# Sinkhorn-sorted block attention with a SwiGLU block on one core: first weight loads in two pairs, mixing matrices of batches 1 to 3 on GpSimd, and a reordered start

## The chip, the cores and the metric

The kernel runs on one core of one Trainium2 chip. The metric is the device time of one execution in microseconds; three executions took 245.49, 244.75 and 244.44, median 244.75. Engines are named TensorE (PE; its weight loads PEld), VectorE (DVE), ScalarE (ACT), GpSimd (POOL) and SyncE (SP). SBUF is the on-chip working memory, PSUM the accumulators that TensorE writes, in eight banks of 2 KB per partition.

## The reference

There are 4 batches, 8 heads, 768 positions and 64 channels per head. The positions are cut into 8 blocks of 96. An 8x8 matrix P per batch and head is normalised five times by rows and columns, and mixes the blocks of keys and values; attention then runs inside each block. The result is the input of a gated block with 512 inputs and 1536 hidden units.

```python
P = sort_net
for _ in range(5):
    P = np.exp(P - np.max(P, axis=-1, keepdims=True))
    P = P / (np.sum(P, axis=-1, keepdims=True) + 1e-09)
    P = P / (np.sum(P, axis=-2, keepdims=True) + 1e-09)
k_sorted = np.einsum('bhij,bhjcd->bhicd', P, k_b)      # k in 8 blocks of 96
v_sorted = np.einsum('bhij,bhjcd->bhicd', P, v_b)
attn = softmax(scale * q_b @ k_sorted.T)               # 96 x 96 in each block
x = (attn @ v_sorted)                                  # -> 3072 tokens x 512
g, val = x @ w_gate, x @ w_val
out = (g * sigmoid(g) * val) @ w_out
```

## The kernel before

**Tiles.** The rows of one batch are 64 = 8 heads times 8 blocks (`R`), so two sets of rows fill the 128 partitions (`lowr`, `highr`). Inputs are float32 in HBM; GpSimd's DMAs convert them to bf16 on the way. P becomes a mixing matrix per batch: `w_ps` (a PSUM bank, 128 x 8 x 4 x 8, written by 32 small matmuls, L497) holds P of all four batches, and `mix_rows` (L501) multiplies it by a 0/1 mask of heads into `rmix[0]`, `rmix[1]` and `rmix["p"]` (batches 2 and 3). Matmuls with these matrices transpose and mix at once: `k0_chunk` (L280) gives the keys of batch 0, `q0_chunk` (L271) its queries, `v_chunk` (L295) its values; `kq_chunk` (L260) does keys and queries of batch 1 and later. Each chunk fills one PSUM bank (8 columns) or a pair (16), which VectorE or ScalarE then drains to SBUF (`drain`, L242: "v" or "s"). For two of the short key chunks the first 16 of 32 key parts are drained at once and the rest by a second drain (`parts`, `drain_rest`).

**Units.** A unit is a pair of heads and four blocks: `qk` makes eight score matmuls (L334) and the exponentials on ScalarE (`exps`, L345 and L347), `av` (L350) eight matmuls with a column of ones for the sum, then on VectorE a reciprocal (L365) and a product (L367) into `st`. Transposes by TensorE (`x_to`, L375) bring `st` into the layout `xts` that the gates read; ScalarE or VectorE drain them. The first half of batch 0 is four units; when these are transposed (`x_first`, L536) the gated block can begin.

**Gated block.** The tokens come in 8 half batches of 384. For each, 12 blocks of 128 hidden units: `gate` (L408) and `value` (L426), four matmuls of 384 columns each, tanh on ScalarE, two products on VectorE; then `outp` (L440) with w_out. The first two blocks are issued piece by piece in `early` (L546), as the transposed units arrive. The rest is a list (`ffn`, L619) into which the attention of the next half batches is merged at written times (`merge`, L606).

**Order.** The order on TensorE, GpSimd, VectorE and ScalarE is the order of the program in the start (`manual_schedule`, L154), and on all but VectorE later on. PSUM is shared by tags: "a" and "b" are two banks each, "x" one, "gen" three, and a chunk waits until its bank is drained. `w_ps` is in a "gen" bank. `fill` (L477) issues idle matmuls between dependent steps.

**Loads.** GpSimd issues the loads in order, with its own work between: v of batch 0, the identity, q and k of batch 0, three copies of v into `vch` (channels first), then the weights `load_gv(0, 512)` (gate and value, columns 0 to 511, one DMA each, L134), the second part of q (`load_q0(1)`), two more pairs of weight loads, v of batch 1 (`load_v`, L126), keys and queries of batch 1 (four loads, L100), w_out in three loads (L187), the copies of v of batch 1 (L632). At most eight of these DMAs are open; the ninth is issued when the first has landed.

Of the kernel before, what the change touches and what calls it, by code (L numbers as in the profile page):

```python
# [10 lines left out]
BF16 = mybir.dt.bfloat16  # L11
AF = mybir.ActivationFunctionType
ALU = mybir.AluOpType
# [4 lines left out]
def kernel(  # L18
# [11 lines left out]
    nc = tc.nc  # L30

    B, H, S, D = q.shape
    NB = sort_net.shape[-1]
# [10 lines left out]
    R = H * NB  # L44
# [7 lines left out]
    wo_dram = moe_w_out.rearrange("(mc p) f -> p mc f", p=128)  # L52

    const = ctx.enter_context(tc.tile_pool(name="const", bufs=1))
# [19 lines left out]
    wo_sb = [wpool.tile([128, 4, DM], BF16, name=f"wo{n}") for n in range(3)]  # L74
# [24 lines left out]
    def load_groups(tile4, rows, src, lo, hi):  # L99
        nc.gpsimd.dma_start(out=tile4[rows, lo:hi, 0:GC * D],  # L100
                            in_=src[:, lo * GC:hi * GC, :].rearrange("p (s c) d -> p s (c d)", c=GC))

    def kq_tile(b):
        if b not in kq_tiles:
            kq_tiles[b] = nat_tile(natp, f"kq{b}", "nat")
        return kq_tiles[b]
# [4 lines left out]
    def load_k(b, lo, hi):  # L111
        load_groups(kq_tile(b), highr, k_nat[b], lo, hi)
# [5 lines left out]
    def load_q(b, lo, hi):  # L118
        load_groups(kq_tile(b), lowr, q_nat[b], lo, hi)
# [13 lines left out]
    def load_w(sb, dram, lo, hi):  # L133
        nc.gpsimd.dma_start(out=sb[:, :, lo:hi], in_=dram[:, :, lo:hi])  # L134

    def load_gv(lo, hi):
        load_w(wg_sb, wg_dram, lo, hi)
        load_w(wv_sb, wv_dram, lo, hi)

    def copy_v(eng, pair, rows, s, n=4, d0=0, d1=D):  # L140
        cs = slice(s * (C // n), (s + 1) * (C // n))
        dst = vch3[rows, d0:d1, cs]
        src = (dense(v_tiles[0])[rows, cs, d0:d1] if rows == lowr else
               grouped(v_tiles[pair])[rows, s, :, d0:d1])
        if eng is nc.scalar:
            eng.copy(dst, src.transpose([0, 2, 1]))  # L146
        else:
            eng.tensor_copy(dst, src.transpose([0, 2, 1]))  # L148

    ident = const.tile([128, 128], BF16)  # L150
    lowr, highr = slice(0, R), slice(R, 2 * R)
# [7 lines left out]
    halves = (lowr, highr)  # L159
# [5 lines left out]
    def load_q0(t):  # L165
        nc.gpsimd.dma_start(out=q0[t].rearrange("p c d -> p (c d)"), in_=q_runs[0, t])
# [7 lines left out]
    copy_v(nc.gpsimd, 0, lowr, 0)  # L174
    copy_v(nc.gpsimd, 0, lowr, 3)
    copy_v(nc.gpsimd, 0, lowr, 5, 8, 40, D)
    load_gv(0, 512)
    load_q0(1)
    load_gv(512, 1024)
    load_gv(1024, DF)  # L180
    load_v(1, 0, 2)
    load_v(1, 2, 4)
    for lo, hi in ((0, 2), (2, 4)):
        load_k(1, lo, hi)
        load_q(1, lo, hi)
    for n in range(3):
        nc.gpsimd.dma_start(out=wo_sb[n], in_=wo_dram[:, n * 4:(n + 1) * 4, :])  # L187

    rmix = {b: const.tile([128, 2, H, NB], BF16, name=f"rmix{b}") for b in (0, 1, "p")}
    for t in rmix.values():  # L190
# [14 lines left out]
    mask = const.tile([128, H], BF16)  # L205
# [3 lines left out]
    rowreds = [const.tile([BH, NB, 1], FP32, name=f"rowred{it}") for it in range(N_ITER)]  # L209
    colred = const.tile([BH, 1, NB], FP32)  # L210
    p_bf = const.tile([BH, NB, 4, NB], BF16)
    def pair_tile(name, tag):
        return psum.tile([128, 1024], FP32, name=name, tag=tag)

    def bank_tile(name, tag="gen"):
        return psum.tile([128, 512], FP32, name=name, tag=tag, bufs=3 if tag == "gen" else 1)
# [54 lines left out]
    def q0_chunk(t, at, n, eng, tag):  # L271
        dst = kqt_tile(0)[:, GI * C:2 * GI * C].rearrange("p (g t r c) -> p t g r c", g=H2, t=2, c=QC)[:, t]
        tp = chunk_tile("tq0", n // 8, tag).rearrange("p (l g r) -> p l g r", l=n, g=H2)
        for lc in range(n):
            for two in range(2):
                nc.tensor.matmul(tp[two * D:(two + 1) * D, lc], lhsT=q0[t][:, at + lc, :],
                                 rhs=sel[:, two], start=True, stop=True)
        drain(eng, dst[:, :, :, at:at + n], tp.rearrange("p l g r -> p g r l"))

    def k0_chunk(at, n, eng, tag, parts=None):  # L280
        dst = kqt_tile(0)[:, 0:GI * C].rearrange("p (n a c) -> p a n c", a=2, c=HC)
        rm = rmix[0].rearrange("p a (g two) i -> p two a g i", two=2)
        tp = chunk_tile("tk0", n // 8, tag).rearrange("p (l a n) -> p l a n", l=n, a=2)
        for lc in range(n):
            for two in range(2):
                nc.tensor.matmul(tp[two * D:(two + 1) * D, lc].rearrange("p a (g i) -> p a g i", g=H2),
                                 lhsT=k0[:, at + lc, :], rhs=rm[:, two], start=True, stop=True)
        src = tp.rearrange("p l a n -> p a n l")
        if parts is None:
            drain(eng, dst[:, :, :, at:at + n], src)  # L290
            return
        drain(eng, dst[:, :, 0:parts, at:at + n], src[:, :, 0:parts])
        return lambda e: drain(e, dst[:, :, parts:, at:at + n], src[:, :, parts:])

    def v_chunk(b, at, n, eng, tag):  # L295
        rows = slice(0, 128) if b % 2 else lowr
        dst = vt_tile(b // 2)[:, b % 2]
        mix = rmix[b][rows, 0].rearrange("p a b -> p (a b)")
        tp = chunk_tile("tv", n // 8, tag).rearrange("p (l n) -> p l n", n=H * NB)
        for ld in range(n):  # L300
            col = (at + ld) * C
            nc.tensor.matmul(tp[:, ld, :], lhsT=vch[rows, col:col + 128], rhs=mix,  # L302
                             start=True, stop=True)
        drain(eng, dst[:, :, at:at + n], tp[0:C].transpose([0, 2, 1]))
# [45 lines left out]
    def qk(b, u, tag="b"):  # L350
        exps(b, u, *scores(b, u, tag))

    def av(b, u, tag="a"):
        half, g = divmod(u, H2)
        vt = vts[b // 2][:, b % 2].rearrange("p (h i) e -> p h i e", h=H)
        av_ps = pair_tile("av_ps", tag).rearrange("p (two n) -> p two n", two=2)
        o = av_ps.rearrange("p two (i e) -> p two i e", i=4)
        for two in range(2):
            e = es[(b, u)][two]
            for i4 in range(4):  # L360
                nc.tensor.matmul(o[:, two, i4, 0:D + 1], lhsT=e[:, i4 * C:i4 * C + 128],  # L361
                                 rhs=vt[:, 2 * g + two, half * 4 + i4, 0:D + 1],
                                 start=True, stop=True)
        r_sb = ssp.tile([C, 2, 4, 1], FP32, name="r_sb", tag="r")
        nc.vector.reciprocal(r_sb, o[0:C, :, :, D:D + 1])  # L365
        st = ssp.tile([C, 4, 2, D], BF16, name="st", tag="st")
        nc.vector.tensor_tensor(st.rearrange("p i two d -> p two i d"), o[0:C, :, :, 0:D],  # L367
                                r_sb.to_broadcast([C, 2, 4, D]), op=ALU.mult)
        sts[(b, u)] = st
# [105 lines left out]
    idle_ps = bank_tile("idle_ps", "x")  # L475

    def fill(tile, n):  # L477
        for _ in range(n):
            nc.tensor.matmul(tile, lhsT=warm_sb[:, 0:128], rhs=warm_sb, start=True, stop=True)  # L479
# [13 lines left out]
    w_ps = bank_tile("w_ps")[:, 0:NB * B * H].rearrange("p (i b h) -> p i b h", b=B, h=H)  # L493
# [4 lines left out]
                             lhsT=p_bf[:, i].rearrange("p a b -> p (a b)"),  # L498
                             rhs=ident[0:BH, 0:BH], start=True, stop=True)

    def mix_rows(dst, rows, b):  # L501
        nc.vector.tensor_tensor(dst, mask[rows].unsqueeze(2).to_broadcast([R, H, NB]),
                                w_ps[rows, :, b].transpose([0, 2, 1]), op=ALU.mult)

    mix_rows(rmix[0][lowr, 0], lowr, 0)
    mix_rows(rmix[0][highr, 1], highr, 0)
    q0_chunk(0, 0, 16, "s", "b")
    v_chunk(0, 0, 8, "v", "gen")
    v_chunk(0, 8, 8, "s", "gen")
    v_chunk(0, 16, 16, "v", "a")  # L510
    v_chunk(0, 32, 8, "v", "gen")
    v_chunk(0, 40, 16, "s", "b")
    v_chunk(0, 56, 8, "s", "gen")
    q0_chunk(0, 16, 8, "v", "x")
    k0_chunk(0, 16, "s", "a")
    k0_chunk(16, 16, "v", "b")
    rest = [k0_chunk(at, 8, "s", "gen", 2 * NB) for at in (32, 40)]
    for drain_rest in rest:
        drain_rest("v")
    idle_ps = bank_tile("idle_ps", "x")  # L520
    fill(idle_ps, 3)
    qk(0, 0, "a")
    qk(0, 1, "b")
    for b in range(1, B):
        rows = halves[b % 2]
        mix_rows(rmix["p"][rows, b % 2] if b > 1 else rmix[1][rows, 0], rows, b)
    qk(0, 2, "gen")
    fill(idle_ps, 1)
    av(0, 0, "a")
    fill(idle_ps, 2)  # L530
    av(0, 1, "b")
    xts[(0, 0)] = xtp.tile([128, H2, TW], BF16, name="xt0_0", tag="xt")
    qk(0, 3, "mixed")
    av(0, 2, "a")

    def x_first(u, eng, tag):  # L536
        x_ps = xt_tile(tag, 1)[:, 0]
        x_to(x_ps, 0, u)
        drain(eng, xts[(0, 0)][:, u, :], x_ps.rearrange("p a b -> p (a b)"))

    x_first(0, "s", "gen")
    x_first(1, "s", "gen")
    av(0, 3, "b")
    first = {}
# [144 lines left out]
```

## Time and profile before

| what | us |
|---|---|
| median of three executions | 244.75 |
| the profiled execution | 245.05 |
| its span on the core | 243.1 |
| PE busy | 235.9 (97%) |
| DVE busy | 154.7 (64%) |
| ACT busy | 112.6 (46%) |
| POOL busy | 51.2 (21%) |
| DMA, mean over the span | 102 GB/s |

The profile is of one execution; times count from the start of its span. In the slices each digit is a fortieth of the span in tenths of busy time. A timeline line has the start, the length, the engine, the line of the kernel, the operation, the tile written and those read, the shape, a count, and in brackets how long the engine stood idle before and what ended the wait. Lines of one kind on end are merged. GB/s count the bytes as written, in bf16 for the loads. PE is busy while matmuls overlap, so a busy PE is not one at its peak.

### The profile page before, as it was taken

The numbers are of one execution on the slowest core, as the hardware profiler recorded it, in microseconds if no ns is written. First come the engines' busy times: TensorE is split into PE (matmuls) and PEld (weight loads), VectorE is DVE, ScalarE is ACT, GpSimd is POOL, SyncE is SP. The second block draws the span as 40 slices with busy tenths as digits, with TensorE's granted clock in tenths as the row PEclk, the third lists the DMA queues.
The fourth block names the chain that finished last, engine by engine and source line by source line (L and its number), as shares of the span: only waits on it lengthen the run. The fifth ranks groups of instructions, "written<-read, shape, count | busy, mean of one in ns | idle before, by whom it ended". The sixth has DMA issues, their size and how long they took to land.

```text
span 243.1 us, 6156 instructions
## 1 busy us (share of the span) xinstructions
PE 235.9 (97%) x2613; PEld 138.7 (57%) x2613; DVE 154.7 (64%) x326; ACT 112.6 (46%) x191; POOL 51.2 (21%) x45
## 2 busy tenths in 40 slices
PE   8798999999999999999999999999999999999994
PEld 5375666676556556555555565565556555555543
DVE  6686789876665585866855855584576476445700
ACT  3976663486625544455453353254325434332312
POOL 5992229970006089000000000000000000000000
PEclk9999999999999999999999999999999999999999
DMA  5989999999926998553122212012111211110122
GB/s 101 210 121 206 207 212 212 205 210 192 166 78 99 220 176 118 108 107 68 48 73 58 49 47 80 0 59 63 32 43 48 74 36 43 43 43 3 43 86 86
DMA packets 39642, 24.77 MB, mean 102 GB/s; under 512 B 29376, under 2 KB 34368, under 8 KB 39616
## 3 DMA queue, kind: packets, MB, share of 16 engines
q0 software_dynamic: 19632, 14.16, 39.3%
q1 hardware_dynamic: 19840, 10.17, 15.7%
q8 instruction: 20, 0.33, 0.6%
q10 hardware_dynamic: 144, 0.07, 0.1%
q14 instruction: 6, 0.05, 0.1%
HBM read 28.32 MB, written 7.86 MB: 149 GB/s over the span
## 4 chain that ended last, share of the span: by engine, by line
PE 89%; DMA 7%; POOL 2%; DVE 1%; issue 0%; ACT 0%; POOLq 0%
PE v_ps L430 26%; PE g_ps L412 25%; PE o_ps L447 25%; DMA wv_sb<-in_moe_w_val_dram 4%; DMA v<-in_v_dram 3%; PE av_ps L361 3%; PE tkq L266 3%; PE qk L334 3%; POOL vch L148 1%; PE tv L312 1%; PE o_ps L463 1%; PE tv L302 1%; PE v_ps L551 1%; PE g_ps L551 1%; PE x_ps L378 0%
## 5 line engine op out<-in xcount | busy, mean ns | idle before, releaser
L422 DVE SCALAR_TENSOR_TENSOR gs_sb<-th_sb,g_ps 128x384 bf16<-128x384 bf16 x96 | 52.9, 551 | 50.3 <-ACT th_sb L420 47.3
L412 PE MATMUL g_ps<-xt,wg_sb 128*128 128x384 bf16 x376 | 76.6, 326 | 0.1
L430 PE MATMUL v_ps<-xt,wv_sb 128*128 128x384 bf16 x376 | 76.5, 326 | 0.0
L420 ACT ACTIVATE th_sb<-g_ps 128x384 bf16<-128x384 f32 x96 | 47.1, 491 | 56.8 <-PE g_ps L412 54.1
L447 PE MATMUL o_ps<-wo,h 128*128 128x512 bf16 x276 | 64.4, 379 | 0.0
L435 DVE SCALAR_TENSOR_TENSOR h<-v_ps,gs_sb 128x384 bf16<-128x384 f32 x96 | 53.4, 556 | 7.7 <-PE tkq L266 0.5
L412 PEld LDWEIGHTS <-wg_sb 128*128 128x128 bf16 x376 | 34.9, 97 | 23.4
L430 PEld LDWEIGHTS <-wv_sb 128*128 128x128 bf16 x376 | 35.0, 97 | 23.1 <-issue 0.2
L447 PEld LDWEIGHTS <-h 128*128 128x128 bf16 x276 | 26.0, 98 | 28.5
L452 ACT COPY o_sb<-o_ps 128x512 f32<-128x512 f32 x23 | 13.5, 586 | 49.3 <-PE o_ps L447 49.3
L148 POOL COPY vch<-v 64x1536 bf16<-64x1536 bf16 (+2 forms) x11 | 28.7, 2655 | 10.2 <-DMA v<-in_v_dram 10.2
L347 ACT ACTIVATE e_all<-qk 96x768 bf16<-96x768 f32 x30 | 23.2, 801 | 4.3 <-PE qk L334 4.3
L367 DVE TENSOR_TENSOR st<-av_ps,r_sb 96x512 bf16<-96x512 f32 x32 | 21.8, 680 | 0.3
L361 PEld LDWEIGHTS <-e_all 96*128 96x128 bf16 x256 | 11.9, 97 | 4.9 <-ACT e_all L347 0.6
L361 PE MATMUL av_ps<-vt,e_all 96*128 96x65 bf16 x256 | 13.0, 193 | 0.0
L246 ACT CAST vt<-tv 96x1024 bf16<-96x1024 f32 (+1 forms) x11 | 10.1, 931 | 4.7 <-PE tv L312 3.5
L365 DVE RECIPROCAL r_sb<-av_ps 96x8 f32<-96x8 f32 x32 | 6.4, 199 | 7.9 <-PE av_ps L361 7.9
L244 DVE CAST vt<-tv 96x1024 bf16<-96x1024 f32 (+1 forms) x7 | 7.4, 1065 | 2.2 <-PE tv L312 1.8
L479 PE MATMUL idle_ps<-warm_sb 128*128 128x512 bf16 x24 | 7.1, 408 | 0.0
L244 DVE COPY oq_v<-o_ps 128x128 f32<-128x128 f32 x1 | 0.3, 292 | 9.3 <-PE o_ps L463 9.3
L397 POOL DMA_DIRECT2D q_scr<-in_q_dram x2 | 5.6, 2810 | 0.3 <-issue 0.3
L146 ACT COPY vch<-v 64x768 bf16<-64x768 bf16 (+1 forms) x4 | 5.5, 1388 | 0.2 <-DMA v<-in_v_dram 0.2
(83 smaller groups left out, 130.4 us busy)
## 6 DMA issues: line engine op xcount, KB each, us to landing
out_dram<-o_sb SPq DMA_DIRECT2D x23, 256.0 KB, 2.0
v<-in_v_dram POOLq DMA_DIRECT2D x4, 384.0 KB, 13.1
wg_sb<-in_moe_w_gate_dram POOLq DMA_DIRECT2D x3, 512.0 KB, 11.7
wv_sb<-in_moe_w_val_dram POOLq DMA_DIRECT2D x3, 512.0 KB, 13.4
wo<-in_moe_w_out_dram POOLq DMA_DIRECT2D x3, 512.0 KB, 15.9
kqp<-in_k_dram POOLq DMA_DIRECT2D x2, 768.0 KB, 9.4
q_scr<-in_q_dram POOLq DMA_DIRECT2D x2, 768.0 KB, 17.5
v<-in_v_dram POOLq DMA_DIRECT2D x2, 768.0 KB, 9.8
```

The lines of the kernel that those rows point to most:

```text
L148: eng.tensor_copy(dst, src.transpose([0, 2, 1]))
L246: nc.scalar.copy(dst, src)
L347: nc.scalar.activation(e_all[:, n:n + 2, 0:4 * C], wide[0:C, :, 0:4 * C], AF.Exp, scale=scale)
L361: nc.tensor.matmul(o[:, two, i4, 0:D + 1], lhsT=e[:, i4 * C:i4 * C + 128], rhs=vt[:, 2 * g + two, half * 4 + i4, 0:D + 1], start=True, sto ...
L367: nc.vector.tensor_tensor(st.rearrange("p i two d -> p two i d"), o[0:C, :, :, 0:D], r_sb.to_broadcast([C, 2, 4, D]), op=ALU.mult)
L412: nc.tensor.matmul(g_ps, lhsT=wg_sb[:, kc, ts(m, 128)], rhs=xt[:, kc, :], start=(kc == 0), stop=(kc == NKC - 1))
L420: nc.scalar.activation(th_sb, g_ps, AF.Tanh, scale=0.5)
L422: nc.vector.scalar_tensor_tensor(gs_sb, th_sb, 1.0, g_ps, op0=ALU.add, op1=ALU.mult)
L430: nc.tensor.matmul(v_ps, lhsT=wv_sb[:, kc, ts(m, 128)], rhs=xt[:, kc, :], start=(kc == 0), stop=(kc == NKC - 1))
L435: nc.vector.scalar_tensor_tensor(h_tiles[n][:, m, :], v_ps, 0.5, gs_tiles.pop(m), op0=ALU.mult, op1=ALU.mult)
L447: nc.tensor.matmul(o_ps, lhsT=h_w[:, m, ts(t3, 128)], rhs=wo_sb[part][:, m % 4, :], start=(m == 0), stop=(m == NFC - 1))
L452: nc.scalar.copy(o_sb, o_ps)
```

## The change

Five things are changed, all in the start of the program. (1) The first pair of weight loads, columns 0 to 511 of gate and value, becomes two pairs of 256 columns with the second part of q between them. (2) `w_ps` of batches 1 to 3 is copied to SBUF (`w_sb`) by VectorE right after batch 0's two mixing matrices, and GpSimd makes the three other mixing matrices from the copy; before, VectorE made them from PSUM after the second unit's scores. In GpSimd's order they stand behind the loads of v of batch 1, and the loads of k and q of batch 1 and of w_out are moved behind them. (3) The chunks of batch 0 change order, size, bank and drain: the second q chunk moves ahead, the keys' second 16 columns become two chunks of 8 on ScalarE, the first part of the last key chunk is drained by VectorE, and the last value channels (56 to 63) come behind the keys, in bank "x", ahead of the remaining key drains. (4) The idle matmuls are fewer and elsewhere. (5) `av(0, 0)` comes ahead of `qk(0, 2)`, and `av(0, 2)` behind the first unit's transposes.

```diff
@@ -174,17 +174,13 @@
-    load_gv(0, 512)
+    load_gv(0, 256)
     load_q0(1)
+    load_gv(256, 512)
     load_gv(512, 1024)
     load_gv(1024, DF)
     load_v(1, 0, 2)
     load_v(1, 2, 4)
-    for lo, hi in ((0, 2), (2, 4)):
-        load_k(1, lo, hi)
-        load_q(1, lo, hi)
-    for n in range(3):
-        nc.gpsimd.dma_start(out=wo_sb[n], in_=wo_dram[:, n * 4:(n + 1) * 4, :])
@@ -209,6 +205,7 @@
+    w_sb = const.tile([128, NB, B, H], BF16)
@@ -498,40 +495,47 @@
-    def mix_rows(dst, rows, b):
-        nc.vector.tensor_tensor(dst, mask[rows].unsqueeze(2).to_broadcast([R, H, NB]),
-                                w_ps[rows, :, b].transpose([0, 2, 1]), op=ALU.mult)
-
-    mix_rows(rmix[0][lowr, 0], lowr, 0)
-    mix_rows(rmix[0][highr, 1], highr, 0)
+    def mix_rows(eng, dst, rows, w, b):
+        eng.tensor_tensor(dst, mask[rows].unsqueeze(2).to_broadcast([R, H, NB]),
+                          w[rows, :, b].transpose([0, 2, 1]), op=ALU.mult)
+
+    mix_rows(nc.vector, rmix[0][lowr, 0], lowr, w_ps, 0)
+    mix_rows(nc.vector, rmix[0][highr, 1], highr, w_ps, 0)
+    nc.vector.tensor_copy(w_sb[:, :, 1:], w_ps[:, :, 1:])
+    for b in range(1, B):
+        rows = halves[b % 2]
+        mix_rows(nc.gpsimd, rmix["p"][rows, b % 2] if b > 1 else rmix[1][rows, 0], rows, w_sb, b)
+    for lo, hi in ((0, 2), (2, 4)):
+        load_k(1, lo, hi)
+        load_q(1, lo, hi)
+    for n in range(3):
+        nc.gpsimd.dma_start(out=wo_sb[n], in_=wo_dram[:, n * 4:(n + 1) * 4, :])
+
     q0_chunk(0, 0, 16, "s", "b")
     v_chunk(0, 0, 8, "v", "gen")
     v_chunk(0, 8, 8, "s", "gen")
     v_chunk(0, 16, 16, "v", "a")
-    v_chunk(0, 32, 8, "v", "gen")
+    v_chunk(0, 32, 8, "s", "gen")
+    q0_chunk(0, 16, 8, "v", "x")
     v_chunk(0, 40, 16, "s", "b")
-    v_chunk(0, 56, 8, "s", "gen")
-    q0_chunk(0, 16, 8, "v", "x")
-    k0_chunk(0, 16, "s", "a")
-    k0_chunk(16, 16, "v", "b")
-    rest = [k0_chunk(at, 8, "s", "gen", 2 * NB) for at in (32, 40)]
+    k0_chunk(0, 16, "v", "a")
+    k0_chunk(16, 8, "s", "gen")
+    k0_chunk(24, 8, "s", "gen")
+    rest = [k0_chunk(32, 8, "s", "gen", 2 * NB), k0_chunk(40, 8, "v", "gen", 2 * NB)]
+    v_chunk(0, 56, 8, "v", "x")
     for drain_rest in rest:
         drain_rest("v")
-    idle_ps = bank_tile("idle_ps", "x")
-    fill(idle_ps, 3)
+    fill(pair_tile("idle_ps", "b")[:, 0:512], 2)
     qk(0, 0, "a")
     qk(0, 1, "b")
-    for b in range(1, B):
-        rows = halves[b % 2]
-        mix_rows(rmix["p"][rows, b % 2] if b > 1 else rmix[1][rows, 0], rows, b)
+    idle_ps = bank_tile("idle_ps", "x")
+    fill(idle_ps, 1)
+    av(0, 0, "a")
     qk(0, 2, "gen")
     fill(idle_ps, 1)
-    av(0, 0, "a")
-    fill(idle_ps, 2)
     av(0, 1, "b")
     xts[(0, 0)] = xtp.tile([128, H2, TW], BF16, name="xt0_0", tag="xt")
     qk(0, 3, "mixed")
-    av(0, 2, "a")
@@ -539,6 +543,7 @@
     x_first(0, "s", "gen")
+    av(0, 2, "a")
     x_first(1, "s", "gen")
     av(0, 3, "b")
```

## The prediction

> **What bounds the kernel now.** First the page's slices (40 slices of 6.08 us, busy tenths).
>
> ```profile
> PE   8798999999999999999999999999999999999994
> DVE  6686789876665585866855855584576476445700
> PEclk9999999999999999999999999999999999999999
> DMA  5989999999926998553122212012111211110122
> ```
>
> TensorE is full from the fifth slice on, at the full granted clock, and DMA is full from the third to the ninth. From about 26 us TensorE runs one written order without holes, so a microsecond won ahead of it is a microsecond of span, unless a later wait gives it back. The change touches only what lies ahead; next therefore the timeline of TensorE there (start, length, operation, count, idle before).
>
> ```profile
> 17.53 0.92 PE L334 MATMUL qk<-kqt 64*128 64x96 bf16 x24
> ...
> 18.77 0.42 PE L361 MATMUL av_ps<-vt,e_all 96*128 96x65 bf16 x8
> ...
> 21.48 0.32 PE L551 MATMUL g_ps<-xt,wg_sb 128*128 128x384 bf16 x1
> 22.39 0.34 PE L551 MATMUL v_ps<-xt,wv_sb 128*128 128x384 bf16 x1 [0.58 <-DMA wv_sb<-in_moe_w_val_dram]
> 22.56 0.34 PE L378 MATMUL x_ps<-ident,st 96*128 96x96 bf16 x4
> ...
> 23.46 0.33 PE L378 MATMUL x_ps<-ident,st 96*128 96x96 bf16 x4
> ...
> 25.46 0.32 PE L276 MATMUL tq<-sel,qk 128*64 128x64 bf16 x8
> ```
>
> The first value matmul waits for wv_sb, and queued behind it are the transposes of units 2 and 3. VectorE had their inputs (st) at 21.82 and 22.66, so unit 3's transpose at 23.46 is late through the weights alone. VectorE before it:
>
> ```profile
> 16.16 1.89 DVE L244 CAST kqt<-tk 128x1024 bf16<-128x1024 f32 x3 [0.31 <-PE tk L286]
> 18.07 0.23 DVE L502 TENSOR_TENSOR rmix<-mask,w_ps 64x64 bf16<-64x64 bf16 x1
> 18.31 0.45 DVE L502 TENSOR_TENSOR rmixp<-mask,w_ps 64x64 bf16<-64x64 bf16 x2
> 19.23 0.20 DVE L365 RECIPROCAL r_sb<-av_ps 96x8 f32<-96x8 f32 x1 [0.46 <-PE av_ps L361]
> ```
>
> The three mixing matrices end 0.46 us before av_ps comes: they delay nobody. Last, GpSimd's timeline, the landings of wg_sb and wv_sb after issue, and two later places where TensorE is not far behind a supplier.
>
> ```profile
> 12.79 0.79 POOL L134 DMA_DIRECT2D wg_sb<-in_moe_w_gate_dram  x1
> 13.56 0.76 POOL L134 DMA_DIRECT2D wv_sb<-in_moe_w_val_dram  x1
> 14.31 0.55 POOL L166 DMA_DIRECT2D qk<-in_q_dram  x1
> ...
> 36.96 0.74 POOL L187 DMA_DIRECT2D wo<-in_moe_w_out_dram  x1 [0.87 <-DMA v<-in_v_dram]
> 37.74 11.24 POOL L148 COPY vch<-v 64x1536 bf16<-64x1536 bf16 x4
> ```
> ```profile
> DMA to landing us min/median/max: 6.8/11.7/15.3
> DMA to landing us min/median/max: 8.8/13.4/18.0
> ```
> ```profile
> 30.40 0.81 PE L430 MATMUL v_ps<-xt,wv_sb 128*128 128x384 bf16 x4
> 50.23 0.63 PE L302 MATMUL tv<-rmix,vch 128*128 128x64 bf16 x16
> ```
>
> With the issue times: first wg_sb lands at 19.56, first wv_sb 22.34, second wv_sb 29.05. The matmul at 30.40 is the first to read that second part (1.3 us spare); the one at 50.23 needs GpSimd's four copies, which end at 48.92 (1.26 us spare).
>
> **The weights in two pairs.** By the packet records the queue moves 1024 B packets at 200 per us over 16 engines (79.8 ns each on its engine), 3072 B at 68 (235), 128 B at 1220 (13.1). A line through the first and last, 3.6 ns + 0.0744 ns/B, gives 232 for the third, so it holds. The new 512 B packets cost 41.7 ns; 2048 of them for 1024 old ones: 85.4 - 81.7 = 3.7 us over 16 engines, delta = 0.23 us later for everything behind. Ends: 0 (cost by bytes) and 5.1 us (512 B priced like 1024 B: 81.7/16). I take 0.23, as four sizes lie on its line.
> The first pair is now as many bytes as the first wg_sb alone: wv_sb lands at about 19.7 instead of 22.34. Issues: two more of 0.76 us on GpSimd, each far ahead of the bytes it queues. Only eight DMAs are ever open (each late issue waits for the landing eight before); counted through, every later issue waits for the same bytes as before, so all from the second gate pair on move by delta only.
> The Trainium skill (DMA: Bandwidth & Descriptors, Anatomy of one DMA) prices a GpSimd DMA at about 2.0 us + bytes/436e3; two more in series would be +4.0 us and a slower kernel. Landings at 26.54, 29.05 and 31.62 stand 2.5 us apart, which is 524 KB at 207 GB/s with no fixed part left, so I take nothing for it.
>
> **Mixing matrices on GpSimd.** VectorE loses 0.67 us that nobody waited for: gain 0. It gains a copy of 128x192 at 12.34; between the 64x64 row (0.22) and the 128x256 drain (0.415), at 1.06 ns per element 0.35. It ends at 12.69, before the first value drain can start (12.73): cost 0, at most 0.03. It frees w_ps's bank at 12.7 instead of 18.76, a third bank for the chunks. GpSimd's products show in no row: 0.25 (its select) to 2.8 us each (64x1536 copy), I take 0.5 by the 64x288 copy (0.66). They stand behind the second v issue (about 22.4) and ahead of the seven issues of k, q, wo (4.6 us); the last wo issue only becomes possible at 36.9, and the queue has bytes until 38.5. Even 8.4 us fits: cost 0.
> The Trainium skill (GPSIMD Engine Reference, Engine selection) sends elementwise products to VectorE, about 2x slower for two inputs on GpSimd. At 0.45 us each the sum stays as it is.
>
> **Drains reordered.** I walk the new order with the old durations (VectorE holds 1.14 us for a 1024 drain, 0.60 for 512, 0.33 for 256; ScalarE 0.91, 0.48, 0.27; matmuls 29 ns value, 16 ns k and q). VectorE: value 0 at 12.73, value 16 at 13.43, q to 15.17; k 0 has its bank at 14.70, is done at 15.40, drained 15.44 to 16.67. ScalarE: q to 13.31, value 8, value 32 to 14.26, value 40 14.51 to 15.42, k 16 from 15.68 to 16.27, k 24, k 32's first half to 17.03. The chunk k 40 waits for k 16's bank (16.27), is done at 16.77, its first half drained by VectorE at 17.23. Then qk(0,0) can start at 17.37 instead of 17.53: 0.16 earlier. Value 56 (to 17.83) and the rests (to 18.49) now stand behind the keys on VectorE; av(0,0) waits for its exp until 18.56, qk(0,2) starts at 18.87, so neither sees them. Ends: 0.15 later (k 40's drain behind value 56 by half its time) to 0.4 earlier (third bank and fewer fills pay in full).
>
> **Units and first gates.** exp(0,0) 17.76 to 18.56, av(0,0) 18.62, VectorE's reciprocal at 19.07 (was 19.23); its four rounds of 0.84 us end unit 3's st at 22.51 (was 22.66). The exps follow at 18.47, 19.25, 20.00. av(0,2), now behind the first transposes, runs at 20.2, ahead of VectorE's turn at 20.75: cost 0. The first value matmul (21.45) finds its weights. What is late next is st and the x bank, drained of unit 2 by ScalarE at 22.57: unit 3's transpose runs at 22.62 instead of 23.46. Gain 0.84; with qk(0,0) unmoved still 0.69.
>
> **Does it last.** The value matmuls come to 29.56, their weights land at 29.05 + 0.23; the q loads of batch 1 land at 41.65 + 0.23, wanted at 42.4; GpSimd's copies end at 49.15, wanted at 49.39. Each holds, the last by 0.24 us: it caps the gain at 1.26 - delta.
> Sum: -0.84 us. The profiled execution took 245.05 (span 243.1 and 1.95 around it), giving 244.2; the median is 0.30 below it: **243.9 us**.
>
> **Rivals.**
> *Small packets cost like large ones* (slower). Delta 5.1 us: the copies would end at 54.0 and the chunk at 50.23 comes 3.8 us late: 248.6. It decides from delta 1.26 us, 50 ns per 512 B packet. The 128 B row (13.1) speaks against it; that no 512 B row exists, for it.
> *The weights come no sooner.* First wg_sb's bytes at 207 GB/s would be through 2.4 us before its landing; if a small DMA's landing trails its bytes as far and more, wv_sb lands after 22 us and only a little is left: 244.3 to 244.8. That the first wg_sb, equal in bytes, landed at 19.56 speaks against it.
> *More is won.* If qk(0,0) comes 0.4 earlier, and delta is near 0, the gain is 1.1 to 1.26 us, where the copies cap it: 243.5. The third bank speaks for it, the two bank waits in my walk against it.
>
> **How the numbers follow.** Forecast 0.52 (own range 243.6 to 244.3), weights no sooner 0.15, small packets 0.14, more won 0.19. A measurement tells 0.5%, 1.2 us. Faster by more: the last case and the forecast's edge with the scatter of the runs (244.44 to 245.49), 0.25; slower 0.14; the rest, 0.61, within. The range runs from the cap with scatter (243.1) past no gain (245.2).
>
> **What would show it.** Right: no wait of the first value matmul for wv_sb, unit 3's transpose near 22.6, first w_ps copy under 0.42 us, the gates of the stream from 25.5, tv of batch 1 at 49.4. Wrong: a hole before the value matmuls near 29.6 or before tv, behind GpSimd's copies; qk(0,0) after 17.6; 512 B packets over 50 ns.

## The result and the profile after

The changed kernel took 245.34 us (median of 12, 245.15 to 245.85), the kernel before beside it 244.58 us (median of 12, 244.31 to 245.49). The ratio is 1.0029, with a 95% interval of 1.0019 to 1.0039: slower by 0.76 us. The prediction was 243.9 us, and its range ended at 245.2.

The profiled execution of the changed kernel took 245.19 us. Its slices (40 of 6.07 us, busy tenths) look like those of before.

```profile
span 242.8 us, 6133 instructions
...
PE   6798999999999999999999999999999999999994
...
PEclk9999999999999999999999999999999999999999
DMA  5999999999937997453122112012111211110122
```

TensorE is as full and its clock as high. The span of 242.8 us is even shorter than the 243.1 of the profile before, though the kernel is slower. Two things must therefore be kept apart: what lies around the span, and which execution of before is the yardstick. Next TensorE's timeline in the changed kernel (start, length, operation, count, idle before).

```profile
17.26 0.38 PE L476 MATMUL idle_ps<-warm_sb 128*128 128x512 bf16 x1 [0.16 <-issue]
17.57 0.52 PE L331 MATMUL qk<-kqt 64*128 64x96 bf16 x16
...
18.82 0.42 PE L358 MATMUL av_ps<-vt,e_all 96*128 96x65 bf16 x8 [0.41 <-ACT e_all L344]
...
21.67 0.32 PE L556 MATMUL g_ps<-xt,wg_sb 128*128 128x384 bf16 x1
21.84 0.32 PE L556 MATMUL v_ps<-xt,wv_sb 128*128 128x384 bf16 x1
...
22.90 0.33 PE L375 MATMUL x_ps<-ident,st 96*128 96x96 bf16 x4
...
24.91 0.95 PE L273 MATMUL tq<-sel,qk 128*64 128x64 bf16 x48
25.79 0.50 PE L409 MATMUL g_ps<-xt,wg_sb 128*128 128x384 bf16 x2
```

The first value matmul no longer waits for its weights, and unit 3's transpose comes at 22.90 instead of 23.46. Against the profile of before that is a gain of 0.55 us up to the gates' stream (the first gate matmul of the list behind `early`, at 25.79 us here and 26.34 there). But the kernel before, run again, shows in another execution (the same view):

```profile
17.55 0.92 PE L334 MATMUL qk<-kqt 64*128 64x96 bf16 x24
...
21.50 0.32 PE L551 MATMUL g_ps<-xt,wg_sb 128*128 128x384 bf16 x1
21.66 0.32 PE L551 MATMUL v_ps<-xt,wv_sb 128*128 128x384 bf16 x1
...
22.82 0.33 PE L378 MATMUL x_ps<-ident,st 96*128 96x96 bf16 x4
...
24.82 0.95 PE L276 MATMUL tq<-sel,qk 128*64 128x64 bf16 x48
25.70 0.50 PE L412 MATMUL g_ps<-xt,wg_sb 128*128 128x384 bf16 x2
```

Here no wait stands before the first value matmul: the first wv_sb landed at 20.86 us, not at 22.34. This is the usual execution. Of 147 executions of the kernel before that stood beside the experiments, 46 have a span of 243.0 us or more; most of the rest lie at 242.3 to 242.8. (Four slow ones, at a granted clock near 0.985, are left out.) The profile that the prediction was made from is one of the late ones.

Against the usual execution the change loses in three places, in us:

| place | before | after | loss |
|---|---|---|---|
| first mixing product (VectorE, 11.86 and 11.84) to the gates' stream | 13.84 | 13.94 | 0.10 |
| gates' stream to the first key chunk of batch 1 (42.62 and 42.92) | 16.92 | 17.13 | 0.21 |
| time outside the span (median) | 1.93 | 2.44 | 0.51 |

The three add up to 0.82 us, the difference of the two profiled executions (245.19 and 244.37); by the medians it is 0.76.

The second place is seen in the changed kernel's chain of waits (start, length, what).

```profile
24.65 0.33 PE v_ps L556 x2
24.98 0.64 PE tq L273 x32
25.62 0.01 issue
25.63 0.56 DVE h L432
26.19 0.47 DVE gs_sb L419
...
26.76 0.56 DVE h L432
27.32 0.61 DVE kqt L241
27.92 0.05 issue
27.97 0.52 PE qk L331 x16
28.48 0.02 issue
28.50 0.81 PE v_ps L427 x4
```

VectorE's first h product, its second gate and h product and its drain of the query chunk have become the path that TensorE's next scores wait for (27.97). VectorE's own timeline shows why:

```profile
24.56 0.56 DVE L419 SCALAR_TENSOR_TENSOR gs_sb<-th_sb,g_ps 128x384 bf16<-128x384 bf16 x1 [0.94 <-ACT th_sb L417]
25.63 0.56 DVE L432 SCALAR_TENSOR_TENSOR h<-v_ps,gs_sb 128x384 bf16<-128x384 f32 x1 [0.52 <-PE tq L273]
```

The h product needs v_ps (complete at 24.34 by the semaphore) and gs_sb (25.15, the wait for it done at 25.18). It starts 0.46 us after that. The releaser that the profile names, the query chunk, is a guess from a nearby end; the product does not read it. In the kernel before (before_again) the same product starts 0.11 us after gs_sb ends:

```profile
24.48 0.55 DVE L422 SCALAR_TENSOR_TENSOR gs_sb<-th_sb,g_ps 128x384 bf16<-128x384 bf16 x1 [0.94 <-ACT th_sb L420]
25.14 0.56 DVE L435 SCALAR_TENSOR_TENSOR h<-v_ps,gs_sb 128x384 bf16<-128x384 f32 x1
```

The third place is after the last instruction of the span. The view of the DMA queues over 243 to 245 us of the changed kernel:

```profile
DMA packets 1, 0.01 MB, mean 4 GB/s; under 512 B 0, under 2 KB 0, under 8 KB 0
...
q14 instruction: 1, 0.01, 1.5%
```

One packet of 8 KB of instructions is fetched at 243.84 us, 1.1 us behind the span's end. In the kernel before, over 242.5 to 244.5 us:

```profile
DMA packets 0, 0.00 MB, mean 0 GB/s; under 512 B 0, under 2 KB 0, under 8 KB 0
```

### The profile page after: what moved, and what is told of

The parts are those of the page before. It is cut to its first block, busy times and chain, and to the rows that moved or that the text cites. A ratio compares the mean times of both kernels' runs of the same rounds, so it can differ in the third digit from the quotient of the medians.

```text
span 242.8 us, 6133 instructions
## 1 busy us (share of the span) xinstructions
PE 233.2 (96%) x2587; PEld 138.7 (57%) x2611; DVE 154.8 (64%) x325; ACT 112.5 (46%) x191; POOL 53.7 (22%) x50
## 4 chain that ended last, share of the span: by engine, by line
PE 90%; DVE 4%; DMA 2%; ACT 1%; issue 1%; DVEq 0%; POOLq 0%
PE v_ps L427 25%; PE g_ps L409 25%; PE o_ps L444 24%; PE av_ps L358 3%; PE tkq L263 3%; PE qk L331 3%; DMA v<-in_v_dram 2%; PE tv L309 1%; PE o_ps L460 1%; PE tv L299 1%; DVE vt L241 1%; DVE h L432 1%; PE g_ps L556 1%; PE idle_ps L476 1%; ACT vch L146 1%
## 5 line engine op out<-in xcount | busy, mean ns | idle before, releaser
L444 PE MATMUL o_ps<-wo,h 128*128 128x512 bf16 x254 | 61.4, 379 | 1.5 <-issue 0.5
L476 PE MATMUL idle_ps<-warm_sb 128*128 128x512 bf16 x20 | 5.7, 382 | 0.4 <-issue 0.4
```

Of the source, the lines that this page charges most:

```text
L444: nc.tensor.matmul(o_ps, lhsT=h_w[:, m, ts(t3, 128)], rhs=wo_sb[part][:, m % 4, :], start=(m == 0), stop=(m == NFC - 1))
```

## The experiments

"Outside" is the median time outside the span. "List" is the number of instructions that the program gives an engine, waits and the closing barrier included; positions count from 0. The profile shows one instruction fewer of each list: 68 on GpSimd where the list has 69, and the h product of the changed kernel as number 63 on VectorE where the list has it at 64. The ratio is to the kernel before run beside each group of experiments, where the late executions were 6 of 35 in one group and 16 of 35 in another; so it does not follow from the median alone.

| run | edit | time, us | ratio to before | span | outside |
|---|---|---|---|---|---|
| before_again | none | 244.37 | 0.9997 [0.9983, 1.0011] | 242.4 | 1.93 |
| pairs_alone | before, weight pairs | 244.86 | 1.0014 [0.9996, 1.0033] | 242.75 | 2.14 |
| one_pair | change, one weight pair | 245.06 | 1.0019 [1.0004, 1.0034] | 242.9 | 2.16 |
| pool_list_longer | before, 6 more on GpSimd | 245.05 | 1.0006 [0.9976, 1.0035] | 242.6 | 2.44 |
| dve_one_more | change, 1 more on VectorE | 245.10 | 1.0032 [1.0018, 1.0046] | 242.7 | 2.39 |
| pool_list_short | change, GpSimd's list at 63 | 244.90 | 1.0010 [0.9999, 1.0021] | 242.95 | 1.94 |
| no_fill | change, 2 idle matmuls fewer | 245.06 | 1.0021 [1.0012, 1.0029] | 242.65 | 2.45 |
| short_lists_no_fill | the three together | 244.50 | 1.0002 [0.9987, 1.0016] | 242.55 | 1.93 |
| before_dve_one_more | before, 1 more on VectorE | 244.51 | 0.9994 [0.9978, 1.0010] | 242.6 | 1.94 |
| before_pool_64 | before, 1 more on GpSimd | 245.16 | 1.0030 [1.0006, 1.0054] | 242.8 | 2.39 |
| before_pool_58 | before, 5 fewer on GpSimd | 244.61 | 0.9997 [0.9975, 1.0020] | 242.65 | 1.96 |
| short_lists_units_as_before | short_lists_no_fill, scores of unit 2 first | 244.75 | 0.9994 [0.9974, 1.0014] | 242.85 | 1.94 |
| before_dve_one_less | before, 1 fewer on VectorE | 245.32 | 1.0025 [1.0004, 1.0046] | 243.4 | 1.92 |
| late_weights_whole | before, q ahead of the weights | 247.73 | 1.0124 [1.0095, 1.0154] | 245.8 | 1.95 |
| late_weights_pairs | the same, weight pairs | 244.55 | 0.9999 [0.9987, 1.0010] | 242.4 | 2.13 |
| before_q_first_pairs | the same, shorter GpSimd list | 244.68 | 1.0004 [0.9996, 1.0013] | 242.6 | 2.07 |
| change_q_first_short | short_lists_no_fill, q ahead of the weights | 244.41 | 0.9980 [0.9961, 0.9999] | 242.5 | 1.93 |

**Which part loses.** The kernel before once more:

> The kernel before, unchanged, for the spans behind its times. In the two profiles the time outside the span is 1.94 us before (245.05 less 243.11) and 2.42 after (245.19 less 242.77), and only after does a code fetch of 8 KB start behind the last instruction. Theory 'tail' (0.48 us of the loss lies outside the span): here time less span is 1.9 to 2.0 us in every execution, spans near 242.6 at the median of 244.58. Rival 'all inside': time less span varies by itself around 2.2, and the spans of the two kernels differ by the whole 0.76 us.

It gave the usual execution shown above. Next the weight pairs alone:

```diff
-    load_gv(0, 512)
+    load_gv(0, 256)
     load_q0(1)
+    load_gv(256, 512)
```

> The kernel before with the two smaller weight pairs alone. My prediction's reading (the weights were the wait): no wait for wv_sb, unit 3's transpose near 22.75, the gates' stream 0.5 to 0.7 us earlier, time 0.5 us under before. Rival 'the wait was a rarity of the one profiled execution' (it was 0.5 us over the median of its kernel): time within 0.15 us of before, or over it by delta 0.2 us. Theory 'tail': GpSimd's list is two instructions longer, time less span 1.9 if the boundary lies beyond them.

Nothing was won, since the wait that the pairs remove is not there in the usual execution. In the profiled execution, a late one of 246.2 us, the first wv_sb landed at 19.83 us, and the lateness had moved to the weights of columns 512 to 1023, whose wv_sb landed at 30.80 us (view of the waits of TensorE, 20 to 60 us):

```profile
PE v_ps L431 <- DMA wv_sb<-in_moe_w_val_dram: 0.8, 1, 0.8
PE x_ps L379 <- DVE st L368: 0.3, 1, 0.3
PE tkq L267 <- DMA kq<-in_q_dram: 0.2, 1, 0.2
```

The change with the first weights as one pair:

```diff
-    load_gv(0, 256)
+    load_gv(0, 512)
     load_q0(1)
-    load_gv(256, 512)
```

> The changed kernel with the first weight pair whole again (columns 0 to 511, then the second part of q). If the pairs carry the gain: a wait for wv_sb of about 0.5 us comes back and the time is 0.5 us over the changed kernel, 245.8. If the wait in the profile of before was a rarity: same as the changed kernel, 245.3. Theory 'tail' (GpSimd's list is two instructions shorter than in the changed kernel, four longer than before): 2.4 us outside the span if the boundary lies within those four, 1.95 otherwise.

Most of the loss stays without the pairs: the median is 245.06 us instead of 245.34, and the 0.28 us are those outside the span (2.16, at a list of 67). In its profile the first wv_sb landed at 21.94 us, and the gates' stream came 14.21 us behind the first mixing product and not 13.94; in such an execution the pairs pay about 0.26 us. The hole of 0.46 us on VectorE is there too (h product at 25.80). Six idle GpSimd instructions at the end of the kernel before:

```diff
+    pad = const.tile([1, 1], BF16)
+    for _ in range(6):
+        nc.gpsimd.memset(pad, 0.0)
```

> The kernel before with six memsets of one element at the end of GpSimd's list, over 100 us before the end, where GpSimd has nothing left to do. Theory 'tail by the length of GpSimd's list': span as before, time less span 2.4 us, time 0.45 us over before. Rival 'tail by something else in the change': time less span 1.95 us, time as before.

The time outside the span became 2.44 us, that of the changed kernel, with GpSimd's list as long as the changed kernel's (69 instead of 63) and everything else as before. Its span was that of before.

**The three prices, each taken back.** One VectorE instruction more in the changed kernel:

```diff
+    one = const.tile([1, 1], BF16)
+    nc.vector.memset(one, 0.0)
     ident = const.tile([128, 128], BF16)
```

> The changed kernel with one more VectorE instruction at the start of its list, a memset of a single element that nothing reads. Measured so far: in the changed kernel VectorE's first h product starts at 25.63 us, 0.46 us after everything it waits for, and it is the 65th instruction of VectorE's list there (position 64, counted from 0); in the kernel before position 64 was a wait on a semaphore, and no such hole was seen. Theory (the list): the hole belongs to the position. With one instruction more, position 64 is a semaphore wait that VectorE reaches while it is busy anyway; the first h product starts near 25.2, the way from the first gate of the stream to the first batch-1 key chunk is 16.9 us and not 17.1, the span falls by 0.2 us (242.9 to 242.7), the time from 245.34 to 245.1. Rival (the bank): the hole comes from the PSUM bank that the product reads while TensorE writes the query chunk; banks are unchanged here, so it stays at 0.46 us and the time at 245.3. The time outside the span stays at 2.4 us in both, GpSimd's list being unchanged.

VectorE's timeline now:

```profile
24.54 0.55 DVE L421 SCALAR_TENSOR_TENSOR gs_sb<-th_sb,g_ps 128x384 bf16<-128x384 bf16 x1 [0.94 <-ACT th_sb L419]
25.20 0.56 DVE L434 SCALAR_TENSOR_TENSOR h<-v_ps,gs_sb 128x384 bf16<-128x384 f32 x1
```

An instruction that does nothing took the hole away, and 0.25 us of the time (245.10 us): the h product follows after 0.11 us, and from the stream to batch 1's keys it is 16.97 us and not 17.13. GpSimd's list at 63 in the changed kernel (the batch 1 copies in two, those of batches 2 and 3 in one, the last two loads of w_out in one):

```diff
-    for n in range(3):
-        nc.gpsimd.dma_start(out=wo_sb[n], in_=wo_dram[:, n * 4:(n + 1) * 4, :])
+    for lo, hi in ((0, 4), (4, 12)):
+        nc.gpsimd.dma_start(out=wo_all[:, lo:hi], in_=wo_dram[:, lo:hi, :])
...
-    for s in range(4):
-        copy_v(nc.gpsimd, 1, both, s)
+    nc.gpsimd.tensor_copy(vch3[both].rearrange("p d (s c) -> p d s c", c=GC),
+                          grouped(v_tiles[1])[both].rearrange("p s c d -> p d s c"))
```

> The changed kernel with GpSimd's list cut from 69 to 63 instructions, the length that the kernel before has: the four copies of the values of batch 1 become two, the four of batches 2 and 3 become one, and the second and third load of the output weights one. Same bytes, same order. Theory (the list): the time outside the span goes with the length of GpSimd's list (1.93 us at 63, 2.12 at 65, 2.17 at 67, 2.44 at 69), so it falls from 2.44 to about 1.93; no instruction fetch (DMA queue 14) near 243.8; time 245.34 to 244.85. Rival (something else in the change makes the end longer, for instance how the loads are spread over the queues): it stays at 2.4 and 245.3. The merged copies of batch 1 must end before the first of that batch's value chunks at 49.9 (they ended at 49.3 in four); should the merged form be slower per element, a hole on TensorE appears there and the span grows by as much.

Outside fell from 2.44 to 1.94 us, no instruction packet came after the span, and the span stayed. The two merged copies took 11.13 us, the four 11.30. Without the idle matmuls ahead of the first scores:

```diff
-    fill(pair_tile("idle_ps", "b")[:, 0:512], 2)
     qk(0, 0, "a")
```

> The changed kernel without the two idle matmuls ahead of the first scores. In the changed kernel the last key drain that these scores need ended at 17.23 us, but the two idle matmuls kept TensorE until 17.47 and the scores began at 17.57. Theory (the idle matmuls set the time): scores at 17.35 to 17.40, and what follows 0.1 to 0.2 us earlier up to the gates' stream (25.79 to 25.6), time 245.34 to 245.2. Rival (the exponentials on ScalarE or VectorE's chain set it): the gates' stream begins at 25.8 as before, time 245.3; or TensorE's granted clock falls a little after the idle stretch, and the time rises by 0.1.

In the profiled execution the whole start lay later, its first mixing product at 12.08. Counted from there the scores came after 5.53 us (changed kernel 5.73, before 5.69) and the stream after 13.74 (13.94, 13.84): 0.20 us won. TensorE's timeline shows that it now waits for VectorE's key drain, as the prediction's walk had it:

```profile
16.93 0.41 PE L299 MATMUL tv<-rmix,vch 64*128 64x64 bf16 x8
17.61 0.52 PE L331 MATMUL qk<-kqt 64*128 64x96 bf16 x16 [0.27 <-DVE kqt L241]
```

All three edits together:

> The three edits together: one more VectorE instruction, GpSimd's list at 63, no idle matmuls ahead of the first scores. If the three prices are right and add up: outside the span -0.50, the hole -0.21, the start -0.1 to -0.2, so 245.34 to 244.45 (244.3 to 244.6), level with the kernel before (244.58). If the lists are not the cause, 245.2 to 245.3.

The prices add up: 245.34 became 244.50, level with the kernel before. Nothing of the change's loss is left over.

**Whose hole it is.** One VectorE instruction more in the kernel before (the same memset as above):

> The kernel before with one more VectorE instruction at the start of its list (a memset of one element that nothing reads). It moves every later VectorE instruction by one: position 64 of the list, a semaphore wait in the kernel before, becomes the first gate product. Theory (the position in the list): a hole of 0.46 us with no wait behind it now appears in this kernel, ahead of the first gate product near 25.0 us, and as the h product and the stream stand behind it, the way from the stream's first gate to the first batch-1 key chunk grows from 16.92 to 17.1 us or a little more; time 0.2 to 0.4 us above the kernel before, 244.75 to 244.95. Rival (the hole belongs to the changed order, its PSUM banks or its drains, and the added instruction in the changed kernel took it away by chance): no hole here, time as the kernel before, 244.5.

No hole appeared, so the theory as written there fell: position 64 is now the first gate product, which waits 0.94 us for ScalarE in any case, so that a stop ahead of it would be covered; no run shows that stop by itself. By this reading, what has to stand at position 64 is an instruction behind a wait that ends late. One instruction fewer puts the h product there:

```diff
-    for pair in range(B // 2):
-        vt_tile(pair)
+    vt_tile(0)
...
     nc.vector.tensor_copy(rmix[1][lowr, 1].rearrange("p h i -> p (h i)"), ident[lowr, lowr])
+    vt_tile(1)
```

> The kernel before with one VectorE instruction fewer ahead of the gates: the memset of the ones column for the second pair of batches stands behind the start and not at its head. Position 64 of VectorE's list is now the first h product, and ahead of it stands a wait on a semaphore, as in the changed kernel; work, order on the other engines and PSUM banks are those of the kernel before. Theory (the sequencer stops for 0.46 us when it comes to position 64, and it shows only where what stands ahead is a wait that ends late, since else work already issued covers it; so nothing was seen with one instruction more, where position 64 was the first gate product, which waits 0.94 us for ScalarE in any case): a hole of 0.46 us ahead of the first h product, at 25.6 us and not 25.1; from the stream's first gate to the first batch-1 key chunk 17.13 us and not 16.92; time 0.2 us above the kernel before, 244.7 to 244.8. Rival (the hole belongs to the changed order or its banks): no hole, time as the kernel before.

VectorE's timeline of that run, and TensorE's:

```profile
24.50 0.55 DVE L421 SCALAR_TENSOR_TENSOR gs_sb<-th_sb,g_ps 128x384 bf16<-128x384 bf16 x1 [0.94 <-ACT th_sb L419]
25.57 0.56 DVE L434 SCALAR_TENSOR_TENSOR h<-v_ps,gs_sb 128x384 bf16<-128x384 f32 x1 [0.52 <-PE tq L275]
```
```profile
27.91 0.52 PE L333 MATMUL qk<-kqt 64*128 64x96 bf16 x16
28.93 0.81 PE L429 MATMUL v_ps<-xt,wv_sb 128*128 128x384 bf16 x4 [0.51 <-DVE gs_sb L421]
```

The hole of 0.46 us is in the kernel before now, with its own order and its own PSUM banks: it belongs to the position. From the stream to batch 1's keys it is now 17.62 us and not 16.92. The 0.70 us (245.32 us in all, where 244.7 to 244.8 was expected) are more than the hole, since a value matmul waits 0.51 us for a gate product that took longer (0.75 us and not 0.54) beside the moved memset (0.17 us). The memset's share was not separated.

**Where GpSimd's list begins to cost.** One memset more at the end of GpSimd's list in the kernel before, and the merged copies in the kernel before:

> The kernel before with one more GpSimd instruction at the end of its list (a memset of one element): 64 instead of 63. It tells where the longer time outside the span begins. Theory with a bound at 63 to 64 (a further fetch as soon as the list passes 63): 2.05 to 2.15 us outside the span, as at 65. Rival (it grows evenly from 63 to 69, 0.08 us an instruction): 2.0.

> The kernel before with the merged copies of the values (batch 1 in two, batches 2 and 3 in one): GpSimd's list at 58 instead of 63. Theory with a bound at 63: nothing more to win, 1.93 us outside the span, time as the kernel before (244.5). Rival (the time outside goes evenly with the length): 1.93 less five times 0.08, 1.5 us, time 244.1. The merged copies should end as the separate ones did, with no hole ahead of batch 1's value chunks.

Outside by length of GpSimd's list: 58: 1.96; 60: 2.07; 63: 1.93; 64: 2.39; 65: 2.13; 67: 2.16; 69: 2.44. A packet of instructions after the span is there from 64 on and in no list up to 63. So it is a step at 64, of 0.2 to 0.5 us, and not a slope; the runs differ in other things too, but 63 and 64 only in one idle memset. Why 64 costs more than 65, and 60 more than 63, is open.

**The order of the units.**

```diff
-    av(0, 0, "a")
     qk(0, 2, "gen")
+    av(0, 0, "a")
```

> The changed kernel with the short lists and without the two idle matmuls, and with the scores of unit 2 put back ahead of the first weighted sum, as in the kernel before. In the changed order TensorE stands 0.36 to 0.41 us before the first weighted sum, waiting for the exponentials. Theory (VectorE's four rounds of reciprocal and product set the time, as the prediction walked it): the scores fill the hole, the first weighted sum and the gates' stream come where they came (13.74 us behind the first mixing product), time 244.5. Rival (TensorE's holes there cost): stream 0.1 to 0.3 us sooner, 244.2 to 244.4, faster than both kernels.

Neither expectation held. The stream came after 13.89 us, 0.15 later than in short_lists_no_fill: the scores of unit 2 read keys that `drain_rest` brings, now behind value channels 56 to 63 on VectorE, so TensorE stood 0.29 us before these scores and the first weighted sum came later. The new order of the units belongs to the new order of the drains.

**Late weights on purpose.** The kernel before with the second part of q ahead of the first weights, whole and then in pairs:

```diff
-    load_gv(0, 512)
     load_q0(1)
+    load_gv(0, 256)
+    load_gv(256, 512)
```

(In late_weights_whole the two added lines are one, `load_gv(0, 512)`.)

> The kernel before with the second part of q loaded ahead of the first pair of weights and not behind it, so that the first weights come late in every execution: the queue had moved all three by 23.85 us, so wv_sb lands near 23.7 and not 20.9. Theory of the prediction (a late first wv_sb holds up the first value matmul and the transposes behind it, and all that follows, one for one): the first value matmul at 23.7 and not 21.7, unit 3's transpose near 24.8 (22.8), the time 1.9 to 2.1 us above the kernel before, 246.4 to 246.7. Rival (the later waits, for batch 1's keys and values, take most of it up): under 1 us above.

> As the run with late whole weights, but with the first pair of weights cut into two pairs, as the change does. Theory: the first wv_sb lands 2.4 us sooner, near 21.3, so the first value matmul does not wait (21.7) and the late load costs nothing; time that of the kernel before and 0.2 us for GpSimd's list of 65 (2.12 us outside the span and not 1.93), 244.7. So where weights are late, pairs are worth 1.7 to 1.9 us, and the prediction's mechanism was right though the wait is not there in the usual execution. Rival (small DMAs land as late as large ones): wv_sb after 22.5 us, time 245.5 or more.

TensorE's timeline with whole weights:

```profile
21.64 0.32 PE L551 MATMUL g_ps<-xt,wg_sb 128*128 128x384 bf16 x1
24.14 0.34 PE L551 MATMUL v_ps<-xt,wv_sb 128*128 128x384 bf16 x1 [2.18 <-DMA wv_sb<-in_moe_w_val_dram]
...
25.21 0.33 PE L378 MATMUL x_ps<-ident,st 96*128 96x96 bf16 x4
```

and in pairs:

```profile
21.58 0.32 PE L552 MATMUL g_ps<-xt,wg_sb 128*128 128x384 bf16 x1
21.74 0.32 PE L552 MATMUL v_ps<-xt,wv_sb 128*128 128x384 bf16 x1
...
22.89 0.33 PE L379 MATMUL x_ps<-ident,st 96*128 96x96 bf16 x4
```

Counted from the first mixing product, late weights pass on one for one (stream after 16.10 us instead of 13.84, and batch 1's keys after 33.01 instead of 30.76), and pairs take all of it away. The profiled execution took 246.77 us; the other three with whole weights took 247.64 to 248.46, at a granted clock of 0.993 instead of 0.999, and their further 0.9 to 1.7 us are not explained here. The prediction's mechanism is right; in the usual execution the wait was not there to be removed.

**Towards a better kernel.** q first, pairs and short lists, in the kernel before (`before_q_first_pairs`) and in the changed one (`change_q_first_short`, where only `load_q0(1)` moves ahead of short_lists_no_fill's weights):

> The kernel before with three edits that the runs so far point to: the second part of q ahead of the weights, the first weights in two pairs, and the values' copies merged (GpSimd's list 60 long). Theory: from the first mixing product to the end 230.57 us, as measured with late weights in pairs, 1.93 us outside the span, and no execution 0.7 us late, as none of ten was there: 244.3 to 244.4, 0.2 us under the kernel before's median (244.5 to 244.6) and 0.4 under its mean. Rival (late executions come from something else, and were missing there by chance): about a third of the executions above 245.

> The changed kernel with short lists, without the two idle matmuls, and with the second part of q ahead of both weight pairs. Theory: from the first mixing product to the end 230.47 us, as without that move, and fewer late executions: 244.2 to 244.4. Rival (its second query chunk or its weights now come at a worse time): 244.5 or more, as without the move.

The second has the lowest ratio to the kernel before of all runs here, 0.9980 [0.9961, 0.9999]: 244.41 against 244.58 us by medians, 244.38 against 244.75 by means, since the late executions are missing. Its interval ends just under 1, and it is one of 17 runs, so the gain is not beyond doubt. In the three kernels with q first and pairs none of 33 executions had a span over 242.9 us, where about a third of the kernel before's had 243.0 or more. That the first weights' landing is what makes those late is supported by this and by two late profiles, that of before and that of before_dve_one_more (wv_sb at 22.38 us, a wait of 0.52 us, span 243.1); for the executions without a profile it is not shown. The first of the two kernels missed its 244.3 to 244.4: its time outside was 2.07 us at a list of 60, and its median span of 242.6 us is that of the kernel before beside it.

## Why the prediction was wrong

- **"Unit 3's transpose at 23.46 is late through the weights alone", and so "Gain 0.84"**: this was true of the execution in the profile and not of the usual one, where it stands at 22.82 with no wait. The step that took most of the 0.84 us failed here: about 0.7 us was counted as a gain on a wait of 0.58 us that, by their spans, about two thirds of the executions do not have. The sum then subtracted the 0.30 us between the profiled execution and the median, and so counted this lateness twice. That first wv_sb landed at 22.34 us in one profile of the kernel and at 20.86 in the other; the times of 244.44 to 245.49 could have warned of such a spread.
- **"Then qk(0,0) can start at 17.37"**: the walk of the drains was right to the hundredth (VectorE's key drain ended at 17.23), but the two idle matmuls that the change puts ahead of the scores were left out of it. The one on record started at 17.26, and the scores came at 17.57, within the bound of 17.6 that the prediction had set. All behind them was late by as much: the first weighted sum came at 18.82 (18.62 in the prediction), unit 3's transpose at 22.90 (22.62). Without them (no_fill) the scores came 5.53 us behind the first mixing product and not 5.69, as early as predicted; but the stream came only 0.10 us sooner than in the kernel before (13.74 and 13.84).
- **The lists.** No term of the sum, and no rival, priced the instructions as such. "Issues: two more of 0.76 us on GpSimd, each far ahead of the bytes it queues" was right for the span. But six more GpSimd instructions (two loads, three products, a wait) cost 0.51 us outside it, and VectorE's list, one shorter, put the h product on position 64, for 0.21 us. These two make almost the whole loss.
- **Delta, "I take 0.23".** The term was mis-sized. Its line was drawn through two packet sizes and held for a third, not for four. In the half microseconds in which the queue carried 512 B packets alone they moved at 326 to 352 per us (means of the ten runs with pairs), 45 to 49 ns each over 16 engines where 41.7 was predicted. Two small for one large (79.8 ns) are then 11 to 18 ns more, 0.7 to 1.2 us for 1024 pairs over 16 engines. (The single records last longer, 62 to 65 ns and 98 to 101 for 1024 B, since they overlap.) Against usual executions the second wv_sb landed about 1.2 us later, at 29.5 to 29.8 us instead of 28.2 to 28.6; with q ahead of both pairs it was 28.24, 28.85 and 29.58 us in three runs, so the order counts too. The term was too small by a factor of three to five. It cost nothing in the usual execution, because the spare there was 1.5 us (value matmul at 29.76, landing 28.24) and not the 1.3 read from the late one; 0.6 us is left of it. That the pairs move the risk to the next weights is seen in pairs_alone.
- **Mixing matrices on GpSimd** cost nothing, as said: the products took 0.32 and twice 0.35 us (taken: 0.5), VectorE's copy 0.36 (0.35), ending at 12.68 (12.69). The Trainium skill (GPSIMD Engine Reference, Engine selection) has about 2x slower than VectorE for two inputs; the trace has 0.32 to 0.35 against 0.23, but VectorE read `w_ps` from PSUM and GpSimd its bf16 copy in SBUF, so the work is not quite the same.
- **"Does it last"** held: no hole before the value matmuls or before tv at 49.88 us. Its margin was misread by little: the copies of before ended at 48.99 us, not 48.92, so 0.17 us and not 0.24 were left by that sum. Nor is DMA full "from the third to the ninth" slice but, by the digits shown, from the fourth to the eleventh; nothing rests on it.

## What to carry to other kernels

A wait on a DMA in one profiled execution is a sample: compare its landing with the spread of the times, and take the gain only for the share of executions that have it, never together with the difference of that execution to the median. Count the instructions that a change adds to or takes from each engine's list as a cost of its own, and look outside the span. Where an engine stands still although all it waits for is done, shift its list by one idle instruction and see whether the hole goes; here that, merged copies and two idle matmuls fewer gave back 0.84 us.

## What the hardware showed that was not expected

- VectorE stopped for 0.46 us at position 64 of its list, when what stood there came behind a wait that ended late: in the changed kernel, in all its variants with that list, and in before_dve_one_less (458 to 465 ns). With the list shifted by one it was gone. In the 14 profiles without the stop (0.11 to 0.12 us from gs_sb to h) the first 8 KB instruction packet inside the span came at 15.7 to 19.5 us; in the five with it (0.52 us), at 28.7 to 29.1. What that packet has to do with the stop, and for which engine it is, the trace does not say.
- The Trainium skill (Runtime: NRT & Kernel Launch, Instruction fetch mechanics) describes refills of 16 KiB, 256 instructions, that go on while the engine executes and are mostly hidden. The instruction packets here are of 16 KB on one queue and 8 KB on another. The 8 KB packet behind the span came with 0.2 to 0.5 us that nothing hid; whether the stop at 64 is such a refill no run shows.
- The time outside the span, 1.93 us with up to 63 instructions on GpSimd apart from the 2.07 at 60, was 2.1 to 2.4 from 64 on.
